# Loading the second pair's keys: two loads of four blocks at steps 5 and 6, then two blocks at every third step

## The chip, the cores and the metric

The kernel runs on one core of one Trainium2 chip. A time is the device time of one execution in microseconds (us). The engines are PE (TensorE, matrix multiplications and transposes), DVE (VectorE), ACT (ScalarE), POOL (GpSimd) and SP (SyncE, which here only starts DMAs). Each engine works through its own list of instructions in order.

## The reference, cut to what matters

Block-sparse attention on 4 batches of 8 heads, 768 positions, 64 channels per head, followed by a token mix:

```python
scores = (q @ k.T) / 8                      # 24 x 24 blocks of 32 x 32 positions
mask = |block_i - block_j| <= 1, or i or j is the first or the last block, or j is one of 3 sampled blocks of i
attn = softmax(where(mask, scores, -1e9))   # x = attn @ v, heads side by side: (4, 768, 512)
theta = x @ w_theta
y = w_tok_r @ (x * cos(theta)) + w_tok_i @ (x * sin(theta))
u = x + y
out = u + relu(u @ w_ch)
```

## The kernel before, in words

**Two pairs.** The four batches are worked as two pairs (`bp` 0 and 1), two batches at a time. A pair has 28 units: six wide units `w` for the two edge rows of blocks, which see all keys (thirds `t` = 0, 1, 2 of the keys, eight blocks each, and two halves `a` of the heads), and then 22 inner units `i` = 1 to 22, one per other row of blocks, each of which sees eight blocks of keys. Unit numbers run through both pairs: 0 to 5 wide and 6 to 27 inner for the first, 28 to 33 wide and 34 to 55 inner for the second.

**Steps.** One loop over `n` runs the units as a pipeline whose order is written by hand. Step `n` does the scores of unit `n + 1` (PE, line 331 for wide and 339 for inner units, tiles `S_w` and `S`), the transposes of unit `n` (line 369, `T_w`, `T`), the products with the values of unit `n - 1` (line 393, `X_w`, `X`), and around them the minimum on DVE (line 342), the exponentials on ACT (line 359) and the normalisation on DVE (lines 400 to 402). Between these, DVE and ACT turn the float64 weights of the token mix into pairs of float32 (lines 63 to 86; the raw weights are loaded from ACT's queue, line 59).

**Keys.** A pair's keys are one tile of 24 blocks (`k0`, `k1`; 128 partitions, 256 float32 per block). The wide units read it directly: a wide unit of third `t` needs blocks `8t` to `8t + 7`. For an inner unit, POOL copies its window and two sampled blocks into `kg` (lines 297 and 276) and ACT the third sampled block (line 279), three steps ahead. The sampled blocks are found by number, so these copies wait for all loads of the tile. The first pair's keys are loaded ahead of the loop. The second pair's tile `k1` has a place of its own and is filled during the first pair's steps by `load_k` (line 231), from SP's queue.

**Values.** For an inner unit the window's rows come into `va` (line 309, SP) and the sampled rows by an indirect DMA into one of four buffers `vb` (line 313, POOL). The second pair's wide units have their values loaded into these same four `vb` buffers by `load_wide` (line 235, SP): two at step 26, two at step 28 and two more at step 30.

**SP's order.** Within a step SP starts, in this order: queries (line 241), window rows (309), a finished result (421), a part of the edge rows' result (438), `load_k`, the edge queries `qe` (257, at step 24), `load_wide`. DMAs of SP and of ACT take the next of eight completion semaphores in turn and wait, when they are started, until the last DMA on that semaphore has landed.

**After the attention** comes the token mix (lines 582 to 702), which is one dense stream of matrix multiplications.

Of the kernel before, what the change touches and what calls it, by code (L numbers as in the profile page):

```python
# [183 lines left out]
def attention(tc, qT, qE, kT, vr, sampled, xs, ident, early_pieces, late_pieces, first_places, follow, spares):  # L184
# [14 lines left out]
    with ExitStack() as ctx, ExitStack() as early:  # L199
# [20 lines left out]
        def make_places(bp):  # L220

            if bp == 0:
                k, v = first_places()
                wide[bp] = [v[:, 1040 * c : 1040 * (c + 1)] for c in range(6)]
            else:
                k = kp.tile([P, 6144], F32, name="k1")
                wide[bp] = vbs + vbs[:2]
            ks[bp] = k.rearrange("r (s g f) -> r s g f", s=NB, g=8)

        def load_k(bp, s0, n, queue=nc.sync):  # L230
            queue.dma_start(ks[bp][:, s0 : s0 + n].rearrange("r s g f -> r s (g f)"), kT[bp][:, s0 : s0 + n])

        def load_wide(bp, t, queue=nc.sync):
            for c in (2 * t, 2 * t + 1):
                queue.dma_start(wide[bp][c], vr[768 * bp + 128 * c : 768 * bp + 128 * c + 128])

        def load_q(bp, i):
            if i % 2 == 0:
                return
            t = qp.tile([P, 2, 2, 4, 32], F32, tag="q", name=f"q{bp}_{i}", bufs=Q_BUFS)  # L240
            nc.sync.dma_start(t.rearrange("r u b p f -> r u (b p f)"), qT[bp][:, i - 1 : i + 1, :])
            qbs[bp, i], qbs[bp, i + 1] = t[:, 0], t[:, 1]
            unscaled[bp, i] = t.rearrange("r u b p f -> r (u b p f)")
# [8 lines left out]
        def scale_edges(bp):  # L252
            scale(qes[bp].rearrange("r b p f -> r (b p f)"))

        def load_edges(bp):
            qes[bp] = ep.tile([P, 2, 4, 64], F32, tag="qe", name=f"qe{bp}")
            nc.sync.dma_start(qes[bp].rearrange("r b p f -> r (b p f)"), qE[bp])
# [41 lines left out]
        def load_window(bp, i):  # L299
            va, runs = vas[i % 2], fresh(i)  # L300
            if i <= 2:
                nc.sync.dma_start(va[96:128], vr[768 * bp : 768 * bp + 32])
            elif i % 3 < 2:

                runs, rows = [(i + 1, 1)], slice(0, 32 * (i % 3) + 32)
                nc.gpsimd.tensor_copy(va[rows], vas[(i + 1) % 2][rows])  # L306
            for b0, n in runs:
                s0 = 32 * (b0 % 3)
                nc.sync.dma_start(va[s0 : s0 + 32 * n], vr[768 * bp + 32 * b0 : 768 * bp + 32 * (b0 + n)])
# [113 lines left out]
        def join(bp, a):  # L423

            xw, f = xws[a], fs[a].rearrange("r t (e b) -> r t b e", e=2)
            for t in range(3):
                nc.gpsimd.tensor_tensor(xw[:, t], xw[:, t], f[:, t].unsqueeze(3).to_broadcast([P, 2, 2, 65]), op=ALU.mult)
                yield
            for t in range(1, 3):
                nc.gpsimd.tensor_tensor(xw[:, 0], xw[:, 0], xw[:, t], op=ALU.add)  # L430
                yield
            rows = xw.rearrange("r t b e d -> r (t b e d)")[:, 260:516]
            normalised(f"{bp}_a{a}", xw[:, 0], rows.rearrange("r (b e d) -> r b e d", b=2, e=2))
            for s_ in range(2):
                for z in range(2):
                    yield
                    r0, p0 = 64 * s_ + 32 * z, 32 * (2 * a + s_)
                    nc.sync.dma_start(xs[bp, p0 : p0 + 32, (NB - 1) * z].rearrange("r b c -> r (b c)"), rows[r0 : r0 + 32])
# [11 lines left out]
        def do(n, stage, *args):  # L450
            if 0 <= n < len(units):
                stage(units[n], *args)

        def inner(n, stage):
            if 0 <= n < len(units) and units[n][1] != "w":
                stage(*units[n][:2])
# [5 lines left out]
        with tc.manual_schedule():  # L462
            load_edges(0)
            make_places(0)
            load_k(0, 0, 8)
            tab = Tables(nc, cp, sampled)

            nc.vector.memset(first, 0.0)
            nc.scalar.activation(first, first, AF.Exp)
            idle = ps_x.tile([P, P], F32, tag="X", name="idle")  # L470
            for _ in range(WARM):
                nc.tensor.matmul(idle, ident, ident, start=True, stop=True)
            decoder = Decoder(early_pieces + late_pieces, stage, nc.scalar)
            load_wide(0, 0)
            load_k(0, 8, 8)
            load_wide(0, 1)
            load_k(0, 16, 8)
            decoder.load(0, nc.sync)
            load_q(0, 1)
            load_wide(0, 2)  # L480
            decoder.load(1, nc.sync)
            load_q(0, 3)
            make_places(1)
            scale_edges(0)
            do(0, scores)
            making = tab.make(nc, cp)
            next(making)
            do(0, weights)
            steps = len(units) + 1
            for n in range(steps):  # L490
                if n == len(units) - 1:
                    early_s.close()
                    next(follow)


                weight = lambda k: sum(4 if u[1] == "w" else 7 for u in units[5:k])
                due = 3 * len(decoder.pieces) * weight(n) // weight(len(units) - 4)
                due = min(due, 3 * len(decoder.pieces)) - decoder.at
                decoder.first_on_scalar(due)
                do(n + 1, scores)  # L500
                next(making, None)
                inner(n + 4, number_blocks)
                inner(n + 3, gather_window)
                inner(n + 3, gather_keys)
                if due > 0:
                    decoder.on_vector()
                if due > 1 and decoder.at % 3:
                    decoder.on_vector()
                do(n, turn)
                do(n - 1, values)  # L510
                if len(units) - 2 <= n < len(units):
                    next(follow)
                do(n, evict)
                do(n + 1, weights)
                inner(n + 3, gather_key)
                inner(n + 3, scale_q)
                decoder.on_scalar()
                do(n - 1, finish)
                if units[min(n + 6, steps - 2)][:2] not in ((0, 1), (0, 3)):
                    inner(n + 6, load_q)  # L520
                inner(n + 2, gather_values)

                inner(n + 1, lambda bp, i: load_window(bp, i) if i > 2 else None)
                inner(n + 3, lambda bp, i: load_window(bp, i) if i <= 2 else None)
                inner(n - 1, store)

                if n <= len(units) and units[n - 1][1:] in (("w", (2, 0)), ("w", (2, 1))):
                    joins.append(join(units[n - 1][0], units[n - 1][2][1]))
                if n % half > 6 and joins and next(joins[0], joins) is joins:
                    joins.pop(0)  # L530
                if 5 <= n < 29 and n % 2:
                    load_k(1, n - 5, 2)
                if n == 24:
                    load_edges(1)
                if n == half - 3:
                    scale_edges(1)
                for t, step in enumerate((half - 2, half, half + 2)):
                    if n == step:
                        load_wide(1, t)

                if n == len(units) - 4:
                    early.close()
                if len(units) - 6 <= n < len(units):
                    next(follow)
            assert not decoder.left() and not joins, (decoder.left(), joins)
# [285 lines left out]
def sparse_attention_then_token_mix(ctx, tc, qT, qE, kT, vr, sampled, w_theta, w_tok_r, w_tok_i, w_ch, outT):  # L831
# [63 lines left out]
    spares = []  # L895
    follow = token_mix(tc, w, last, xs, outT, bias, n_batch, lambda: spares[0]())
    attention(tc, qT, qE, kT, vr, sampled.bitcast(I32), xs, ident, early, late, first_places, follow, spares)
    for _ in follow:
        pass
# [47 lines left out]
```

## Time and profile before

| | |
|---|---|
| three runs | 593.72, 599.39 and 599.77 us, median 599.39 |
| the profiled execution | 595.23 us, its span 593.5 us |
| mean granted TensorE clock | 0.976 |
| busy over the span | PE 92%, PE weight loads 73%, DVE 72%, ACT 57%, POOL 31% |
| queue of SP and queue of POOL | 53.28 MB and 22.85 MB, 29.0% and 14.3% of the DMA engines' time |
| attention, then token mix | until about 248 us, then 345 us |

A span runs from the first to the last instruction; the execution's own time is 1.7 us more. Busy shares are means over stages that have different limits: in the token mix PE alone is near full, in the attention several engines and the DMA engines are. Line numbers are those of the kernel before; in the changed kernel the lines behind the edit stand three lines lower.

### The profile page before, as it was taken

The page shows a single profiled execution, that of the slowest core. Times are in us where ns is not written, and L with a number is a line of the kernel's source. Part 1 is how long each engine was busy: PE and PEld are TensorE (multiplying, and loading weights), DVE is VectorE, ACT ScalarE, POOL GpSimd, SP SyncE. Part 2 cuts the span into 40 slices and gives each one's busy share as a digit, 9 for nine tenths or more (in the row PEclk, how much of TensorE's full clock was granted, in tenths as well). Part 3 has the DMA queues.
Part 4 walks back from the last instruction along what each step waited for, and adds up shares of the span by engine and source line. Part 5 has one row for each costly group of instructions (what it writes and reads, how often), then busy time and mean ns, then how long its engine had stood idle before and what let it go on. Part 6 is the DMA issues. An engine that isn't in the chain of part 4 may idle for free.

```text
span 593.5 us, 17325 instructions
## 1 busy us (share of the span) xinstructions
PE 547.3 (92%) x7092; PEld 434.5 (73%) x7092; DVE 426.5 (72%) x846; ACT 335.3 (57%) x684; POOL 185.6 (31%) x281
## 2 busy tenths in 40 slices
PE   6997786779988888899999999999999999999997
PEld 4775554556645655688888888888888888888886
DVE  3778998978799989879999995657722659614252
ACT  4798687768967878766474562345530446421220
POOL 1389869922588899520000000000000000000000
PEclk9899989889998989999999999999999999999999
DMA  8979999879987988842333132310202311102002
GB/s 311 351 222 270 263 264 253 251 207 313 273 229 211 260 240 225 227 128 76 85 110 87 36 94 86 104 53 8 83 20 80 99 36 35 36 27 81 1 1 106
DMA packets 53087, 86.67 MB, mean 146 GB/s; under 512 B 5392, under 2 KB 31632, under 8 KB 52624
## 3 DMA queue, kind: packets, MB, share of 16 engines
q1 hardware_dynamic: 43200, 53.28, 29.0%
q0 software_dynamic: 6944, 22.85, 14.3%
q10 hardware_dynamic: 2864, 9.44, 5.2%
q8 instruction: 56, 0.92, 0.7%
q14 instruction: 23, 0.19, 0.1%
HBM read 72.95 MB, written 12.58 MB: 144 GB/s over the span
## 4 chain that ended last, share of the span: by engine, by line
PE 73%; DVE 14%; DMA 6%; issue 3%; ACT 2%; SPq 0%; DVEq 0%; ACTq 0%
PE ya L668 23%; PE yb L668 11%; PE T L369 5%; PE S L339 4%; DVE m L342 4%; PE h L609 4%; PE X L393 4%; PE h L612 4%; PE h L610 4%; PE o L693 3%; PE o L694 3%; PE o L695 2%; PE X_w L393 2%; PE T_w L369 2%; DMA k<-in_kT_dram 2%
## 5 line engine op out<-in xcount | busy, mean ns | idle before, releaser
L359 ACT ACTIVATE P<-S,m 128x256 f32<-128x256 f32 x176 | 70.0, 498 | 15.1 <-DVE m L342 13.9
L369 PE MATMUL T<-ident,P 128*128 128x128 f32 x352 | 61.3, 299 | 16.0 <-ACT P L359 12.6
L369 PEld LDWEIGHTS T<-ident,P 128*128 128x128 f32 x352 | 41.2, 146 | 44.7 <-ACT P L359 35.5
L342 DVE TENSOR_REDUCE m<-S 128x4 f32<-128x1024 f32 x44 | 53.5, 1216 | 9.2 <-PE S L339 7.5
L339 PE MATMUL S<-kg,q 64*32 64x256 f32 x1408 | 54.2, 395 | 5.7 <-issue 5.4
L668 PE MATMUL ya<-w_values,zh 128*128 128x512 f32 x160 | 59.4, 395 | 0.0
L375 ACT COPY pT<-T 128x512 f32<-128x512 f32 x88 | 47.8, 599 | 12.9 <-PE T L369 12.6
L393 PE MATMUL X<-vb,pT 128*32 128x65 f32 (+1 forms) x1408 | 48.2, 227 | 6.9 <-issue 6.9
L393 PE MATMUL X<-va,pT 128*32 128x65 f32 (+1 forms) x1408 | 48.8, 230 | 6.1 <-issue 5.5
L313 POOL DMA_INDIRECT vb<-in_vr_dram,rows x44 | 44.5, 1012 | 19.5 <-PE X_w L393 9.2
L297 POOL COPY kg<-k 128x256 f32<-128x256 f32 (+2 forms) x66 | 37.5, 585 | 33.0 <-DMA k<-in_kT_dram 15.9
L668 PE MATMUL ya<-w_keys,zh 128*128 128x512 f32 x128 | 47.6, 396 | 0.0
L276 POOL COPY kg<-k 128x256 f32 x88 | 46.3, 552 | 0.0
L701 DVE SCALAR_TENSOR_TENSOR of<-o,xT 128x512 f32<-128x512 f32 (+1 forms) x24 | 13.3, 557 | 45.7 <-PE o L695 42.5
L393 PEld LDWEIGHTS X<-va,pT 128*32 128x32 f32 (+1 forms) x1408 | 34.1, 114 | 14.7 <-issue 12.2
L668 PE MATMUL yb<-w_values,zh 128*128 128x256 f32 x160 | 44.6, 278 | 0.0
L393 PEld LDWEIGHTS X<-vb,pT 128*32 128x32 f32 (+1 forms) x1408 | 36.2, 115 | 8.7 <-issue 8.6
L306 POOL COPY va<-va 32x1040 f32<-32x1040 f32 (+1 forms) x28 | 32.5, 1160 | 23.3 <-DMA va<-in_vr_dram 13.6
L609 PE MATMUL h<-w_theta_hi,xh 128*128 128x512 f32 x96 | 38.2, 398 | 0.4 <-ACT xh L598 0.4
L625 DVE SCALAR_TENSOR_TENSOR rr<-t,h 128x512 f32<-128x512 f32 x24 | 16.5, 687 | 29.8 <-ACT t L619 29.8
L610 PE MATMUL h<-w_theta_lo,xh 128*128 128x512 f32 x96 | 37.9, 395 | 0.0
L339 PEld LDWEIGHTS S<-kg,q 64*32 64x32 f32 x1408 | 22.8, 108 | 19.1 <-issue 10.3
(175 smaller groups left out, 1460.0 us busy)
## 6 DMA issues: line engine op xcount, KB each, us to landing
va<-in_vr_dram SPq DMA_DIRECT2D x58, 130.0 KB
q<-in_qT_dram SPq DMA_DIRECT2D x22, 256.0 KB
xs<-xo SPq DMA_DIRECT2D x22, 256.0 KB
xr<-xs SPq DMA_DIRECT2D x22, 256.0 KB
xa<-xs SPq DMA_DIRECT2D x88, 64.0 KB
raw_tok_r<-in_w_tok_r_dram ACTq DMA_DIRECT2D x8, 576.0 KB
out_dram<-of SPq DMA_DIRECT2D x16, 256.0 KB
v<-in_vr_dram SPq DMA_DIRECT2D x6, 520.0 KB
```

Of the source, the lines that this page charges most:

```text
L276: nc.gpsimd.tensor_copy(*sampled_keys(bp, i, k))
L297: nc.gpsimd.tensor_copy(kgs[i % 2][:, s0 : s0 + n], ks[bp][:, b0 : b0 + n])
L313: nc.gpsimd.indirect_dma_start(out=vbs[(i + 1) % VB][rows], out_offset=None, in_=vr, in_offset=bass.IndirectOffsetOnAxis(ap=tab.rows[rows, ...
L339: nc.tensor.matmul(sc[32 * p : 32 * p + 32, e, b, :], q[rows, b, p, :], keys[rows, :, 4 * b + p, :], start=True, stop=True)
L342: nc.vector.tensor_reduce(m.rearrange("r (e b) -> r e b", e=2), sc, axis=AX.X, op=ALU.min)
L359: nc.scalar.activation(pt[:, e, b], sc[:, e, b], AF.Exp, bias=m[:, 2 * e + b : 2 * e + b + 1], scale=-1.0)
L369: nc.tensor.transpose(banks[k // 4][:, k % 4], pt[:, (k // 2) % 2, k % 2, 128 * (k // 4) : 128 * (k // 4) + 128], ident)
L375: nc.scalar.copy(out[:, 4 * h : 4 * h + 4], bank)
L393: nc.tensor.matmul(s["X"][rr, b, e, :], s["T"][0:rows, 4 * c + 2 * e + b, rr], v[0:rows, v0 : v0 + 65], start=c == 0, stop=c == 1,)
L609: nc.tensor.matmul(ps, hi[:, c, :], wh[:, c, :], start=c == 0, stop=False)
L610: nc.tensor.matmul(ps, hi[:, c, :], wl[:, c, :], start=False, stop=False)
L668: nc.tensor.matmul(acc, z[:, dd], wt[:, t0 : t0 + n], start=first and (n == 512 or c % 2 == 0), stop=last, skip_group_check=n == 256,)
```

## The change

Before, `k1` comes in twelve loads of two blocks (256 KB each) at the odd steps 5, 7, ... 27. After, it comes in ten: four blocks (512 KB) at step 5 and four at step 6, then two blocks each at steps 8, 11, 14, 17, 20, 23, 26 and 29. The bytes are the same.

```diff
-                if 5 <= n < 29 and n % 2:
-                    load_k(1, n - 5, 2)
+
+                if n in (5, 6):
+                    load_k(1, 4 * n - 20, 4)
+                if 8 <= n < 32 and n % 3 == 2:
+                    load_k(1, 8 + (n - 8) // 3 * 2, 2)
```

No instruction of PE, DVE, ACT or POOL is added, removed or moved. On SP two DMAs fewer are started and the others change places. At the beginning (steps 5 to 8) SP's list is, before, where `k1` is the second pair's key tile, `q0_7` the first pair's queries and `va` a window of values:

```order
L231 DMA k1_160<-in_kT_dram 128x512
L241 DMA q0_7_629<-in_qT_dram 128x512
L309 DMA va1_117<-in_vr_dram 32x1040
L231 DMA k1_160<-in_kT_dram 128x512
L241 DMA q0_9_823<-in_qT_dram 128x512
L309 DMA va0_116<-in_vr_dram 32x1040
L421 DMA xs_73<-xo0_1_722 128x512
L309 DMA va1_117<-in_vr_dram 32x1040 x2
L231 DMA k1_160<-in_kT_dram 128x512
```

and after:

```order
L231 DMA k1_160<-in_kT_dram 128x1024
L241 DMA q0_7_629<-in_qT_dram 128x512
L231 DMA k1_160<-in_kT_dram 128x1024
L309 DMA va1_117<-in_vr_dram 32x1040
L241 DMA q0_9_823<-in_qT_dram 128x512
L309 DMA va0_116<-in_vr_dram 32x1040
L421 DMA xs_73<-xo0_1_723 128x512
L231 DMA k1_160<-in_kT_dram 128x512
L309 DMA va1_117<-in_vr_dram 32x1040 x2
```

The first two loads are twice as wide, the second has moved ahead of a window load, and the third stands ahead of the next pair of window loads.

At the other end (steps 25 to 30) SP's list is, before, where the `vb` are the values of the second pair's wide units and `q1` the second pair's queries:

```order
L231 DMA k1_160<-in_kT_dram 128x512
L309 DMA va0_116<-in_vr_dram 32x1040
L421 DMA xs_73<-xo0_19_2480 128x512
L438 DMA xs_73<-xw0_w01_346 32x256
L235 DMA vb0_118<-in_vr_dram 128x1040
L235 DMA vb1_119<-in_vr_dram 128x1040
L231 DMA k1_160<-in_kT_dram 128x512
L241 DMA q1_1_2719<-in_qT_dram 128x512
L421 DMA xs_73<-xo0_21_2645 128x512
L235 DMA vb2_120<-in_vr_dram 128x1040
L235 DMA vb3_121<-in_vr_dram 128x1040
L241 DMA q1_3_2837<-in_qT_dram 128x512
```

and after:

```order
L309 DMA va0_116<-in_vr_dram 32x1040
L421 DMA xs_73<-xo0_19_2478 128x512
L438 DMA xs_73<-xw0_w01_346 32x256
L231 DMA k1_160<-in_kT_dram 128x512
L235 DMA vb0_118<-in_vr_dram 128x1040
L235 DMA vb1_119<-in_vr_dram 128x1040
L241 DMA q1_1_2716<-in_qT_dram 128x512
L421 DMA xs_73<-xo0_21_2643 128x512
L235 DMA vb2_120<-in_vr_dram 128x1040
L235 DMA vb3_121<-in_vr_dram 128x1040
L231 DMA k1_160<-in_kT_dram 128x512
L241 DMA q1_3_2835<-in_qT_dram 128x512
```

The last key load, which brings blocks 22 and 23, stood between `vb1` and `vb2`; now it stands behind `vb3`.

On PE the order is the same. At step 31 it reads, before, with the semaphores that each instruction waits for (`DMAHW` are the eight of the DMAs; 7 and 0 are here those of the key loads of steps 27 and 25, 3 and 4 those of `vb2` and `vb3`):

```order
L331 MATMUL S_w_2841<-k_160,qe_2403 64x256 [waits DMAHW7_49,DMAHW0_49,DVE_49]
L331 MATMUL S_w_2841<-k_160,qe_2403 64x256 x7
L369 MATMUL T_w_0_2869<-ident,P_w_2830 128x128 [waits PE_49,Activation_49]
L369 MATMUL T_w_0_2869<-ident,P_w_2830 128x128 [waits Activation_49] x3
L369 MATMUL T_w_1_2870<-ident,P_w_2830 128x128 [waits PE_49]
L369 MATMUL T_w_1_2870<-ident,P_w_2830 128x128 x3
L393 MATMUL X_w_2879<-vb_120,pT_w_2827 64x65 [waits DMAHW3_49,DVE_49]
L393 MATMUL X_w_2879<-vb_120,pT_w_2827 64x65
L393 MATMUL X_w_2879<-vb_121,pT_w_2827 64x65 [waits DMAHW4_49]
```

and after:

```order
L331 MATMUL S_w_2839<-k_160,qe_2401 64x256 [waits DMAHW5_49,DMAHW6_49,DMAHW2_49,DVE_49]
L331 MATMUL S_w_2839<-k_160,qe_2401 64x256 x7
L369 MATMUL T_w_0_2867<-ident,P_w_2828 128x128 [waits PE_49,Activation_49]
L369 MATMUL T_w_0_2867<-ident,P_w_2828 128x128 [waits Activation_49] x3
L369 MATMUL T_w_1_2868<-ident,P_w_2828 128x128 [waits PE_49]
L369 MATMUL T_w_1_2868<-ident,P_w_2828 128x128 x3
L393 MATMUL X_w_2877<-vb_120,pT_w_2825 64x65 [waits DMAHW0_49,DVE_49]
L393 MATMUL X_w_2877<-vb_120,pT_w_2825 64x65
L393 MATMUL X_w_2877<-vb_121,pT_w_2825 64x65 [waits DMAHW1_49]
```

The scores of unit 32, the first of the last third of the keys, now wait for semaphore 2, which is that of the load of step 29; they stand ahead of the product that needs `vb2` and `vb3`.

## The prediction

> **What bounds the kernel now.** I read the page first: PE is busy for 92% of the span, but DMAs can only matter where others wait for them. So the busy times by stage come next (per engine us and count, then granted clock, DMA share, GB/s).
>
> ```profile
> core 0: us, PE busy (x) PEld busy (x) DVE busy (x) ACT busy (x) POOL busy (x), PEclk, DMA share, GB/s
> 26.00:44.00 18.00, 17.91 (x439) 12.64 (x432) 13.14 (x24) 17.74 (x46) 13.04 (x20) 1.00 0.80 231
> 44.00:64.00 20.00, 15.39 (x491) 10.63 (x495) 17.43 (x33) 15.65 (x36) 19.32 (x29) 1.00 0.98 265
> ...
> 132.00:152.00 20.00, 19.54 (x409) 14.36 (x408) 16.52 (x32) 16.82 (x40) 5.04 (x10) 0.91 0.93 297
> 152.00:248.00 96.00, 81.29 (x2201) 54.15 (x2194) 87.57 (x151) 76.51 (x180) 80.56 (x115) 0.96 0.85 236
> 248.00:593.00 345.00, 340.42 (x1960) 291.66 (x1959) 218.75 (x469) 145.74 (x242) 11.65 (x20) 1.00 0.22 66
> ```
>
> The last 345 us are PE's token mix, with DMAs at 0.22; the change cannot touch them except by moving their start. From 152 to 248 us DVE is busy for 91% of the time: it sets the pace there, and DVE time that goes unused just before is not won back. The key loads fall between 26 and 135 us; the two stages at its head have the DMA engines 0.80 and 0.98 occupied. The turn from the first pair to the second, 132 to 152 us, belongs to PE (19.54 of 20 us). The chain that ended last shows where a DMA stands on the path there (start, us, what):
>
> ```profile
> 114.28 8.56 DMA raw_tok_r<-in_w_tok_r_dram
> ...
> 122.85 4.07 DMA qe<-in_qE_dram
> ...
> 140.20 6.73 DMA vb<-in_vr_dram
> ...
> 148.01 1.00 PE S_w L331 x13
> ```
>
> The first piece (weights, then edge queries behind them on one semaphore) is not changed by the edit: neither issue moves past the other. The second is the load of `vb3`, which lands at 146.93 us and is waited for by the product of unit 30.
>
> **The last load, step 29.** These are PE and SP around it, in order of time:
>
> ```profile
> 140.82 1.09 PE L331 MATMUL S_w<-k,qe 64*64 64x256 f32 x16
> 141.84 1.09 PE L369 MATMUL T_w<-ident,P_w 128*128 128x128 f32 x8
> 142.86 1.15 PE L393 MATMUL X_w<-vb,pT_w 128*64 128x65 f32 x32
> 143.94 1.09 PE L331 MATMUL S_w<-k,qe 64*64 64x256 f32 x16
> 144.97 1.27 PE L369 MATMUL T_w<-ident,P_w 128*128 128x128 f32 x8
> ...
> 146.97 1.04 PE L393 MATMUL X_w<-vb,pT_w 128*64 128x65 f32 x28 [0.46 <-DMA vb<-in_vr_dram]
> ```
>
> ```profile
> 133.31 0.42 SPq L231 DMA_DIRECT2D k<-in_kT_dram  x1
> ...
> 139.20 0.33 SPq L421 DMA_DIRECT2D xs<-xo  x1
> 139.70 0.87 SPq L235 DMA_DIRECT2D vb<-in_vr_dram  x2
> 140.67 0.53 SPq L241 DMA_DIRECT2D q<-in_qT_dram  x1
> ```
>
> The scores at 143.94 us are unit 32's, the first that read blocks 16 to 23. Before, their last load was issued at 133.31 us and was in long since. After, it takes the place of the query load at 140.67 us, because SP cannot pass the result store of 139.20 us and the two `vb` loads. The 256 KB then stand behind `vb3` on the same queue. At this stage's 297 GB/s they need 0.88 us, so I put their landing at 146.93 + 0.88 = 147.8 us, and the scores at 147.85 instead of 143.94 us. PE works in order: scores, transposes and the product (1.02 + 1.02 + 1.08 us from the starts at 140.82, 141.84, 142.86 and 143.94) then put the next scores at 150.97 us, against 148.01 in the chain. That is **+3.0 us**. The wait for `vb3` that was there (0.46 us) vanishes into it. Bounds: as fast as the 4.07 us of `qe`, the load would land at 144.7 us, and the product would still wait for `vb3`: 0. As slow as the 8.56 us of the weights, it lands at 149.2 us: +4.4. I take 3.0, because the row nearest to it is `vb3` itself, issued just ahead on the same queue. Behind the waiting scores on PE stand all later scores; DVE's minimum and ACT's exponentials wait for them, and with them the DVE-bound stage.
>
> POOL waits for the same load:
>
> ```profile
> 138.53 0.40 POOL L297 COPY kg<-k 128x256 f32<-128x256 f32 x1 [8.44 <-DMA k<-in_kT_dram]
> ...
> 141.61 1.27 POOL L276 COPY kg<-k 128x256 f32 x2
> 151.31 1.02 POOL L313 DMA_INDIRECT vb<-in_vr_dram,rows  x1 [8.43 <-PE X_w L393]
> ```
>
> Its 4.4 us of copies move from 138.5 to 147.8 us and end at 152.2; the gather behind them moved to about 154.3 with PE, so this costs nothing. ACT's copy of the third sampled block stands behind unit 32's exponentials, which wait anyway.
>
> **The clock after the gap.** PE would stand still for 3.9 us. Stretches of 3.4 us, and what clock the next one had:
>
> ```profile
> 111.50:114.90 3.40, 1.42 (x7) 0.85 (x8) 3.30 (x8) 2.06 (x6) 3.23 (x5) 1.00 0.85 292
> 114.90:118.30 3.40, 3.40 (x91) 2.47 (x97) 3.30 (x7) 3.40 (x9) 2.94 (x6) 0.50 0.93 274
> 125.20:128.60 3.40, 1.51 (x38) 0.89 (x37) 0.36 (x1) 1.66 (x4) 1.23 (x2) 1.00 0.69 169
> 128.60:135.40 6.80, 5.95 (x92) 3.99 (x88) 5.73 (x12) 5.34 (x13) 1.44 (x2) 0.50 0.62 184
> 53.50:56.90 3.40, 1.76 (x81) 1.05 (x71) 2.52 (x6) 3.23 (x8) 3.24 (x6) 1.00 1.04 279
> 56.90:60.30 3.40, 3.37 (x110) 2.44 (x109) 2.59 (x3) 2.12 (x6) 3.40 (x5) 1.00 1.00 325
> ```
>
> With PE busy for 1.42 and 1.51 of 3.4 us the next stretch ran at 0.50; with 1.76 it stayed at 1.00. However a gap of 3.9 us falls across such stretches, one of them has at most 3.4 - 1.95 = 1.45 us of work. So I expect one stretch at half clock, in which a PE that never rests loses half of 3.4 us: **+1.7 us**. Bounds: 0, if PE's stretch hides under ACT, and 3.4, if it lasts for 6.8 us as at 128.60. I take the single stretch, as after 111.50.
>
> The Trainium skill, "TensorE: Matmul & The Clock Gate", Part 1, says that the clock falls to half after at least one idle window of about 3.4 us, and that windows run freely. By that rule a gap of 3.9 us rarely holds a whole window, and the sum would be +2.0 us, the first of the rivals below. The rows at 111.50 and 125.20 speak against it: neither stretch was idle throughout.
>
> **The first loads, steps 5 and 6.** By 28 us 1024 KB are issued where there were 256, 768 KB more, 3.4 us of queue at that stage's 231 GB/s. The second load passes a window load that SP holds back until PE frees its buffer:
>
> ```profile
> 38.62 0.33 SPq L309 DMA_DIRECT2D va<-in_vr_dram  x1
> 38.99 0.95 SPq L231 DMA_DIRECT2D k<-in_kT_dram  x1
> ```
>
> The stage around it, in the columns of the first table:
>
> ```profile
> 34.00:42.00 8.00, 8.00 (x266) 6.06 (x272) 6.30 (x12) 8.00 (x20) 7.06 (x13) 1.00 0.66 178
> ```
>
> Between 34 and 42 us the DMA engines are only 0.66 occupied, 2.7 us free, and the load of 38.99 us is gone; so the burst fits almost whole into a hole. Cost 0; if it does not fit, one stall of PE such as the 1.83 us below: 0 to +1.8.
>
> **The middle, steps 7 to 25.** Ten loads become six, 1024 KB less, and those of steps 8, 14 and 20 pass ahead of window loads. What could be won are PE's stalls for which the profile shows no releaser:
>
> ```profile
> 45.10 1.83 issue
> 46.93 0.50 PE X L393 x18
> ...
> 55.26 1.67 issue
> ...
> 61.92 1.08 issue
> ...
> 96.62 1.86 issue
> ```
>
> SP had issued key loads at 38.99 us (above) and at
>
> ```profile
> 48.23 0.44 SPq L231 DMA_DIRECT2D k<-in_kT_dram  x1
> ...
> 94.16 0.42 SPq L231 DMA_DIRECT2D k<-in_kT_dram  x1
> ```
>
> and the page has of the queues (packets, MB, share):
>
> ```profile
> q8 instruction: 56, 0.92, 0.7%
> ```
>
> The first falls inside a group of equal matmuls (18 of 64 are left at 46.93 us), so no semaphore is late. The instruction queue moved 0.92 MB in the span, so code comes in over the same DMA engines, and I read these stalls as PE waiting for its code behind data. Those at 45.10, 55.26 and 96.62 us come some 2 to 7 us behind a key load that is gone; each could shrink by 256 KB at 265 GB/s, 1.0 us, so at most -3.0, and at least 0, since loads elsewhere move closer to other fetches. I take **-1.0**, one of three. Two DMAs fewer on SP, 0.4 us each, are worth 0: SP mostly waits.
>
> The Trainium skill, "DMA: Bandwidth & Descriptors", Queues, rings and completion order, says that each DMA engine takes turns between queues packet by packet. Then code does not stand behind a backlog of keys, the middle wins nothing, and the sum is 1.0 higher. No row here shows where a fetch stood.
>
> **The sum.** +3.0 + 1.7 + 0 - 1.0 = +3.7 us on the profiled execution's 595.2 us gives 598.9. That execution lies 4.2 us below the median of 599.39; it and the three runs (593.72 to 599.77) have a mean of 597.0, and I predict from there: **600.7 us**. A change within 1%, 6 us, can hardly be told from none here.
>
> **Rivals**, each as a difference from before.
> - *Full clock*: the gap comes without the half clock, or ACT hides it: 3.0 - 1.0 = +2.0, 599.0 us. For it: the limit between 1.51 and 1.76 us of work is read from few stretches. Chance 0.17.
> - *No relief*: a fetch of code does not stand behind keys, so the middle wins nothing: +4.7, 601.7 us. For it: the stall at 61.92 us comes though no key load that goes stands shortly ahead of it. Chance 0.12.
> - *Faster*: the load of step 29 overtakes (0, no half clock), and the three stalls go altogether (1.83 + 1.67 + 1.86): -5.4, 591.6 us. For it: DMAs at 0.98 from 44 to 64 us, where 512 KB leave; against it, a load would have to overtake two on its own queue. Chance 0.12.
> - *Slower*: the burst is late. If PE's code misses its place behind 1 MB around 40 us (+1.8) and a second half-clock stretch follows there (+1.7), with the step-29 wait at its upper end (4.4 + 1.7) and no relief, +9.6, 606.6 us. It decides once the 768 KB take more than the 2.7 free us. Chance 0.19.
>
> **How the numbers follow.** The forecast has 0.40. All but the faster and slower cases lie within 1%; around them a run's scatter of 3 us puts some over. Slower by over 1%: most of the slower case and a little of the forecast and of no relief, 0.23. Faster: two thirds of its case, 0.08. Within: 0.69. The range leaves out about half of the two outer cases: 593.5 to 606.5 us.
>
> **What would show it.** PE's `S_w` of unit 32 waits for `DMA k<-in_kT_dram` for about 4 us near the turn, POOL's wait for the keys grows from 8.4 to about 17 us, and the clock of the next 3.4 us is 0.50. The stalls at 45.10 and 55.26 us shrink or not. I am wrong if unit 32's scores start within 1 us of the transposes' pace, or if a new wait stands between 28 and 44 us.

## The result, and the profile after

| | before | changed |
|---|---|---|
| first comparison, 20 executions each: median | 595.12 us (588.94 to 599.94) | 601.88 us (597.32 to 606.63) |
| mean | 595.26 us | 601.80 us |
| the profiled execution, its span, mean clock | 595.23, 593.5 us, 0.976 | 604.64, 602.9 us, 0.968 |

The ratio (changed over before) is 1.014 with a 95% interval of 1.011 to 1.017. Two later comparisons, each on a chip of its own and run with the experiments below, gave 1.0037 (1.0004 to 1.0071) and 1.0096 (1.0054 to 1.0138). The changed kernel is slower in all three; the size is not steady. The plain mean of the three ratios is 1.009, 5.4 us on 595. Ratios leave disturbed executions out, so they can differ from the quotient of two medians.

The stages of the changed kernel, in the columns of the prediction's first table (busy us of each engine and count, granted clock, DMA share, GB/s):

```profile
core 0: us, PE busy (x) PEld busy (x) DVE busy (x) ACT busy (x) POOL busy (x), PEclk, DMA share, GB/s
26.00:44.00 18.00, 16.67 (x466) 12.12 (x469) 13.12 (x22) 16.69 (x42) 13.62 (x23) 1.00 0.91 291
44.00:64.00 20.00, 14.56 (x360) 9.54 (x360) 14.92 (x31) 13.85 (x34) 16.92 (x26) 0.91 0.82 229
...
132.00:152.00 20.00, 16.24 (x326) 12.30 (x328) 12.30 (x25) 12.61 (x30) 3.35 (x9) 0.87 0.91 304
152.00:248.00 96.00, 75.09 (x2007) 51.18 (x2006) 83.14 (x139) 72.24 (x173) 73.77 (x109) 0.96 0.79 216
248.00:602.00 354.00, 349.59 (x2235) 298.36 (x2233) 227.68 (x487) 153.64 (x261) 16.09 (x25) 1.00 0.23 70
```

The edit's first half shows in the DMA columns: 0.91 instead of 0.80 up to 44 us, 0.82 instead of 0.98 after it. In the same two stages PE is busy for 16.67 us where it was 17.91, and for 14.56 where it was 15.39, and the clock from 44 to 64 us is 0.91 where it was 1.00. At the turn, 132 to 152 us, PE is busy for 16.24 us where it was 19.54, and every other engine is less busy with it. PE, then SP, then POOL around the load of step 29 (start, duration, what, and in brackets the idle time before it and what ended it):

```profile
142.19 1.15 PE L393 MATMUL X_w<-vb,pT_w 128*64 128x65 f32 x32
147.11 1.86 PE L331 MATMUL S_w<-k,qe 64*64 64x256 f32 x16 [3.76 <-issue]
148.90 1.95 PE L369 MATMUL T_w<-ident,P_w 128*128 128x128 f32 x8
...
151.87 1.09 PE L331 MATMUL S_w<-k,qe 64*64 64x256 f32 x16
```

```profile
139.03 0.88 SPq L235 DMA_DIRECT2D vb<-in_vr_dram  x2
139.96 0.57 SPq L231 DMA_DIRECT2D k<-in_kT_dram  x1
```

```profile
147.07 0.40 POOL L297 COPY kg<-k 128x256 f32<-128x256 f32 x1 [16.20 <-DMA k<-in_kT_dram]
...
155.24 1.01 POOL L313 DMA_INDIRECT vb<-in_vr_dram,rows  x1 [4.81 <-PE X_w L393]
```

SP starts the last key load right behind `vb2` and `vb3`. POOL's copy, which waits for all of `k1`, starts at 147.07 us, and unit 32's scores at 147.11 us. The trace names no releaser for the 3.76 us on PE ("issue"), but POOL is released by the key load 0.04 us earlier, and the same wait is put down to the key load in the experiments with that load alone. Behind it, scores and transposes take 1.86 and 1.95 us where they took 1.09: the clock was halved.

```profile
143.88:147.29 3.41, 0.18 (x4) 0.21 (x8) 0.37 (x2) 0.55 (x2) 0.22 (x1) 1.00 1.03 409
147.29:150.71 3.42, 3.42 (x24) 2.23 (x19) 1.63 (x4) 0.58 (x1) 3.13 (x9) 0.50 1.04 298
```

From unit 31's scores to unit 33's it takes 11.72 us (140.15 to 151.87), against 7.12 before (140.82 to 147.94): +4.6 us. The execution is 9.4 us longer than the profiled one of before, so as much again lies elsewhere. PE's waits without a releaser, in total, times and longest, are after

```profile
PE X L393 <- issue: 16.9, 12, 2.8
PE S L339 <- issue: 10.3, 6, 3.7
...
PE T L369 <- issue: 2.8, 1, 2.8
```

and before

```profile
PE X L393 <- issue: 12.5, 11, 2.4
...
PE S L339 <- issue: 5.4, 4, 2.5
```

that is 30.0 against 17.9 us, each of them one execution; the wait for the key load is not counted in. Whether that belongs to the change had to be tested.

### The profile page after: what moved, and what is told of

It is laid out like the page before. It is cut to its first block, busy times and chain, and to the rows that moved or that the text cites. A ratio compares the mean times of both kernels' runs of the same rounds, so it can differ in the third digit from the quotient of the medians.

```text
span 602.9 us, 17322 instructions
## 1 busy us (share of the span) xinstructions
PE 547.8 (91%) x7092; PEld 437.3 (73%) x7092; DVE 424.3 (70%) x846; ACT 334.4 (55%) x684; POOL 177.8 (29%) x281
## 4 chain that ended last, share of the span: by engine, by line
PE 76%; DVE 10%; issue 6%; DMA 3%; ACT 3%; SPq 1%; DVEq 0%; ACTq 0%
PE ya L671 22%; PE yb L671 11%; PE T L369 7%; PE X L393 6%; PE S L339 6%; PE h L612 4%; PE h L615 4%; PE h L613 4%; PE o L696 3%; PE o L697 2%; DMA k<-in_kT_dram 2%; PE o L698 2%; DVE m L342 2%; PE S_w L331 1%; ACT P L359 1%
## 5 line engine op out<-in xcount | busy, mean ns | idle before, releaser
L359 ACT ACTIVATE P<-S,m 128x256 f32<-128x256 f32 x176 | 69.8, 496 | 17.2 <-DVE m L342 16.9
L369 PEld LDWEIGHTS T<-ident,P 128*128 128x128 f32 x352 | 42.5, 151 | 41.6 <-ACT P L359 30.9
L339 PE MATMUL S<-kg,q 64*32 64x256 f32 x1408 | 55.0, 406 | 10.3 <-issue 10.3
L393 PE MATMUL X<-va,pT 128*32 128x65 f32 (+1 forms) x1408 | 50.7, 234 | 9.4 <-issue 9.4
L393 PE MATMUL X<-vb,pT 128*32 128x65 f32 (+1 forms) x1408 | 49.7, 232 | 7.5 <-issue 7.4
L297 POOL COPY kg<-k 128x256 f32<-128x256 f32 (+2 forms) x66 | 36.2, 565 | 47.0 <-DMA k<-in_kT_dram 23.2
L393 PEld LDWEIGHTS X<-va,pT 128*32 128x32 f32 (+1 forms) x1408 | 35.2, 116 | 16.3 <-issue 14.5
L276 POOL COPY kg<-k 128x256 f32 x88 | 41.9, 502 | 0.0
L306 POOL COPY va<-va 32x1040 f32<-32x1040 f32 (+1 forms) x28 | 30.8, 1101 | 27.2 <-DMA va<-in_vr_dram 18.2
```

What stands on the lines that cost most here:

```text
L276: nc.gpsimd.tensor_copy(*sampled_keys(bp, i, k))
L297: nc.gpsimd.tensor_copy(kgs[i % 2][:, s0 : s0 + n], ks[bp][:, b0 : b0 + n])
L339: nc.tensor.matmul(sc[32 * p : 32 * p + 32, e, b, :], q[rows, b, p, :], keys[rows, :, 4 * b + p, :], start=True, stop=True)
L359: nc.scalar.activation(pt[:, e, b], sc[:, e, b], AF.Exp, bias=m[:, 2 * e + b : 2 * e + b + 1], scale=-1.0)
L369: nc.tensor.transpose(banks[k // 4][:, k % 4], pt[:, (k // 2) % 2, k % 2, 128 * (k // 4) : 128 * (k // 4) + 128], ident)
L393: nc.tensor.matmul(s["X"][rr, b, e, :], s["T"][0:rows, 4 * c + 2 * e + b, rr], v[0:rows, v0 : v0 + 65], start=c == 0, stop=c == 1,)
```

## The experiments

**The theory**: the cost is the last key load behind `vb2` and `vb3`, with the half clock that follows. **The rivals**: the burst (the wide loads of steps 5 and 6), or the loads that it moves, make PE's code late; or no part costs anything that can be told from scatter. The kernels came in three groups of four, each on one chip with its own executions of the kernel before.

**First group** (before: median 598.47 us). *The burst without the late load:*

```diff
-                if 5 <= n < 29 and n % 2:
+                if n in (5, 6):
+                    load_k(1, 4 * n - 20, 4)
+                if 13 <= n < 29 and n % 2:
```

> The kernel before, with its first four key loads (steps 5, 7, 9, 11) replaced by two of four blocks at steps 5 and 6; steps 13 to 27 as before. Theory A (the turn alone: the scores of unit 32 wait for the last load, +3.0, and the clock then halves, +1.7): same as before, within 1.5 us. Theory B (the burst of 1 MB makes PE's code late at about 48 us and at 62 us, as in the changed kernel's profile): +2 to +4 us, with a PE stall of over 2.5 us between 40 and 66 us.

Ratio 1.0037 (0.9992 to 1.0081), median 601.39 us: not clear of none.

*The late load without the burst:*

```diff
-                if 5 <= n < 29 and n % 2:
-                    load_k(1, n - 5, 2)
+                if 5 <= n < 27 and n % 2 or n == 29:
+                    load_k(1, min(n, 27) - 5, 2)
```

> The kernel before, with its last key load alone (blocks 22 and 23) moved from step 27 to step 29, behind the loads of vb2 and vb3. Theory A: +4.7 us or the whole measured difference of about 7; POOL's wait for the keys grows to about 16 us, and the scores of unit 32 start 3 to 4 us later than the pace, with the next 3.4 us at clock 0.50. Theory B: at most +2.

Ratio 1.0074 (1.0029 to 1.012), median 602.39 us: slower. At the turn its profiled execution (605.01 us, the longest of its twelve) names the releaser:

```profile
145.18 1.15 PE L393 MATMUL X_w<-vb,pT_w 128*64 128x65 f32 x32
149.23 1.09 PE L331 MATMUL S_w<-k,qe 64*64 64x256 f32 x16 [2.90 <-DMA k<-in_kT_dram]
150.26 1.09 PE L369 MATMUL T_w<-ident,P_w 128*128 128x128 f32 x8
```

Here the wait is 2.90 us instead of 3.76, and the clock stayed full behind it: the groups take 1.09 us.

*The change with its last load back at step 27, ahead of `vb2`:*

```diff
-                if 8 <= n < 32 and n % 3 == 2:
-                    load_k(1, 8 + (n - 8) // 3 * 2, 2)
+                if 8 <= n < 29 and n % 3 == 2 or n == 27:
+                    load_k(1, 22 if n == 27 else 8 + (n - 8) // 3 * 2, 2)
```

> The changed kernel, with its last key load moved back from step 29 to step 27, between vb1 and vb2; all other loads as changed. Theory A: back at before, or up to 1 us under it by the thinner middle. Theory B: still +2 to +4 over before. POOL's wait for keys falls to about 8 us in either.

Ratio 1.0041 (0.9996 to 1.0086), median 601.22 us. The turn is as before: PE waits for no key,

```profile
143.81 1.04 PE L393 MATMUL X_w<-vb,pT_w 128*64 128x65 f32 x28 [0.64 <-DMA vb<-in_vr_dram]
144.77 1.09 PE L331 MATMUL S_w<-k,qe 64*64 64x256 f32 x16
...
147.90 1.09 PE L331 MATMUL S_w<-k,qe 64*64 64x256 f32 x16
```

and unit 32's scores follow unit 31's by 3.13 us. The time, however, did not come back whole: what is left over is -0.2 to +5.1 us.

*The change with 48 more score matmuls ahead of unit 32's scores* (three times the scores of the first third, overwritten by the real ones), to keep PE working in the gap:

```diff
                 q, keys = qes[bp], ks[bp][:, 8 * t : 8 * t + 8]
+                for _ in range(3 if (bp, t, a) == (1, 2, 0) else 0):
+                    for b, s_, e in [(b, p, e) for b, p, e in heads if p < 2]:
+                        rows, p = slice(64 * e, 64 * e + 64), 2 * a + s_
+                        nc.tensor.matmul(sc[...], q[rows, b, p, :], ks[bp][rows, 0:8, 4 * b + p, :], start=True, stop=True)
```

> The changed kernel with 48 extra score matmuls (unit 32's queries on blocks 0 to 7, overwritten by its own scores right after) ahead of unit 32's scores, so that PE works for 3.1 us of the 3.8 that it waits for the last load. Theory A with the clock term: the scores start at the same time, but the clock behind them stays at 1.00, and the time is 1.5 to 2 us under the changed kernel. Rival (the half clock costs nothing since ACT or DVE set the pace there): same as the changed kernel or up to 0.5 us more.

Ratio 1.014 (1.0087 to 1.0192) from eight executions (plain means: 603.08 us against 598.74 before), though at the turn it did what was meant (L332 are the added matmuls, L335 the scores, L373 the transposes):

```profile
143.46 2.82 PE L332 MATMUL S_w<-k,qe 64*64 64x256 f32 x48
147.12 1.09 PE L335 MATMUL S_w<-k,qe 64*64 64x256 f32 x16 [0.84 <-DMA k<-in_kT_dram]
148.15 1.09 PE L373 MATMUL T_w<-ident,P_w 128*128 128x128 f32 x8
...
150.25 1.09 PE L335 MATMUL S_w<-k,qe 64*64 64x256 f32 x16
```

Full clock behind the wait, and 9.92 us from unit 31's scores (140.33) to unit 33's, 1.8 less than the changed kernel's 11.72. The whole time did not show it; it was run again below.

**Second group** (before: median 599.68 us). *The changed kernel once more:*

> The changed kernel once more, on the chip of the next three. Theory A2 (two costs add up: the late load, +4.4 by its run alone, and the burst, +2.4 by the two runs that have it): +6 to +8 over before, clock under 0.95 between 44 and 64 us. Rival (the burst's +0.4% was scatter): +4 to +5.

Ratio 1.0037 (1.0004 to 1.0071), well under the first 1.014. The turn is the same again:

```profile
142.83 1.09 PE L331 MATMUL S_w<-k,qe 64*64 64x256 f32 x16
...
149.96 1.98 PE L331 MATMUL S_w<-k,qe 64*64 64x256 f32 x16 [3.93 <-issue]
151.87 1.73 PE L369 MATMUL T_w<-ident,P_w 128*128 128x128 f32 x8
...
154.61 1.09 PE L331 MATMUL S_w<-k,qe 64*64 64x256 f32 x16
```

*Twice the burst, and no late load:*

```diff
-                if 5 <= n < 29 and n % 2:
+                if n in (5, 6):
+                    load_k(1, 8 * n - 40, 8)
+                if 21 <= n < 29 and n % 2:
```

> The kernel before, with eight blocks at step 5 and eight at step 6 (2 MB) in place of eight loads of two, then two blocks at steps 21, 23, 25 and 27 as before. Theory A2 (a burst delays PE's code): +4 to +8, with longer stalls of PE without releaser between 36 and 66 us than the 1.8 us of before, and the clock halved there. Rival (the burst is free, the hole at 34 to 42 us takes it, or the bytes saved later pay for it): within 1.5 of before.

Ratio 0.9977 (0.9937 to 1.0018), median 598.25 us. Two megabytes in the two loads cost nothing that can be told, and in this execution PE worked through them (same columns as the stages above):

```profile
26.00:34.00 8.00, 7.99 (x162) 5.51 (x152) 4.63 (x10) 7.90 (x22) 3.90 (x6) 1.00 1.03 342
34.00:42.00 8.00, 7.74 (x181) 5.46 (x178) 5.47 (x10) 7.49 (x18) 5.99 (x12) 1.00 0.86 298
```

With the DMA engines full to 34 us PE is busy for 7.99 of 8 us. The +4 to +8 us that the rival of the burst asked for lie outside the interval. A smaller cost is not excluded: this kernel also loads no keys from step 7 to step 20, which could pay for it.

*The kernel before with its last load at step 28, one place ahead of `vb2` and `vb3`:*

```diff
-                if 5 <= n < 29 and n % 2:
-                    load_k(1, n - 5, 2)
+                if 5 <= n < 27 and n % 2 or n == 28:
+                    load_k(1, min(n, 27) - 5, 2)
```

> The kernel before, with its last key load moved to step 28, right ahead of the loads of vb2 and vb3 (in the run with it at step 29 it stood right behind them). Theory A (what costs is standing behind 1 MB on the same queue): unit 32's scores wait for at most 0.5 us, vb3 lands 0.9 us later, the time is 0 to +1.5 over before. Rival (what costs is the later step as such, or the scatter): +3 to +5 as with step 29.

Ratio 1.0006 (0.9964 to 1.0048). Two places on SP's queue separate it from the slower kernel with step 29:

```profile
143.48 0.42 SPq L231 DMA_DIRECT2D k<-in_kT_dram  x1
144.08 0.92 SPq L235 DMA_DIRECT2D vb<-in_vr_dram  x2
```

```profile
148.04 1.09 PE L331 MATMUL S_w<-k,qe 64*64 64x256 f32 x16
...
151.56 1.04 PE L393 MATMUL X_w<-vb,pT_w 128*64 128x65 f32 x28 [1.14 <-DMA vb<-in_vr_dram]
```

Unit 32's scores (148.04 us) wait for nothing: the load was in within 4.56 us of its issue. Behind the two `vb` loads it took 7.15 us in the changed kernel (139.96 to 147.11), so it is the place on the queue that counts, and not the later step. The price is a wait for `vb3` of 1.14 us instead of 0.46.

*All twelve loads at steps 14 to 25:*

```diff
-                if 5 <= n < 29 and n % 2:
-                    load_k(1, n - 5, 2)
+                if 14 <= n < 26:
+                    load_k(1, 2 * n - 28, 2)
```

> The kernel before, with the twelve loads of two blocks at every step from 14 to 25, none ahead. Theory A2 (queues that are full at 26 to 64 us make PE's code late): the stalls between 40 and 64 us shrink, clock there 1.00, time 0 to -3. Rival (DVE sets the pace from 64 us on, so early time is not won, and the loads now crowd the weights and edge queries at 114 to 127 us): 0 to +3, with a longer wait for qe than 5.0 us.

Ratio 1.0039 (1.0000 to 1.0078), no wait for the last load, `vb3` waited for 0.27 us. Nothing gained, perhaps something lost.

**Third group** (before: median 597.88 us), to have the disputed sizes side by side. *The changed kernel a third time, the late load alone again, and the added matmuls again:*

> The changed kernel once more, as the measure for the other three on the same chip. Its ratio to the kernel before was 1.014 the first time and 1.0037 the second. If the cost is the wait at the turn alone (+3 to +4.7 us), the ratio is 1.005 to 1.008; if there is a second cost of the size of the first result, it is above 1.011; if there is none to be measured, it is within 0.003 of 1. In the profile unit 32's scores wait for 2.9 to 3.9 us in every case.

> The kernel before with its last load alone moved from step 27 to step 29. Theory A (the cost of the whole change is this load, which stands behind vb2 and vb3): the same time as the changed kernel on this chip, within 2 us, and 3 to 5 us over the kernel before. Rival B (the two loads of four blocks, or the loads moved between them, cost as well): 2 us or more below the changed kernel. Rival C (nothing that can be measured): within 1.5 us of the kernel before.

> The changed kernel with 48 more score matmuls ahead of unit 32's scores, into the same tile and overwritten by it, so that PE works in the gap. If the half clock after the gap carries 1.7 us of the cost, this kernel is 1.5 to 2 us faster than the changed kernel on the same chip, since the extra work of 2.8 us fits into the wait of 3 to 4 us. If the half clock is hidden under the other engines, it is the same within 1 us. If the extra matmuls don't fit into the wait, it is slower.

Ratios 1.0096 (1.0054 to 1.0138), 1.0083 (1.0044 to 1.0121) and 1.0073 (1.0034 to 1.0112), means 602.56, 601.28 and 600.79 us against 597.49 before. The late load alone is 3.8 us over before and 1.3 us under the whole change, with an uncertainty of 2.1 on the latter. The added matmuls bring 1.8 us against the whole change, also with an uncertainty of 2.1: of the size at the turn, but not resolved. The late load alone, and then the added matmuls, at the turn:

```profile
146.27 1.98 PE L331 MATMUL S_w<-k,qe 64*64 64x256 f32 x16 [3.91 <-DMA k<-in_kT_dram]
148.19 1.76 PE L369 MATMUL T_w<-ident,P_w 128*128 128x128 f32 x8
```

```profile
144.26 2.82 PE L332 MATMUL S_w<-k,qe 64*64 64x256 f32 x48
148.06 1.09 PE L335 MATMUL S_w<-k,qe 64*64 64x256 f32 x16 [0.98 <-DMA k<-in_kT_dram]
```

*A candidate, all keys in by step 19:*

```diff
-                if 5 <= n < 29 and n % 2:
-                    load_k(1, n - 5, 2)
+                if n in (5, 6):
+                    load_k(1, 8 * n - 40, 8)
+                if 13 <= n < 21 and n % 2:
+                    load_k(1, n + 3, 2)
```

> A candidate: eight blocks each at steps 5 and 6, then two each at steps 13, 15, 17 and 19, so that no key load stands among the values of the second pair's wide units at steps 26 to 29. Theory A (only the end of the keys' order matters, and a burst is free): S_w of unit 32 has no wait for k, and the wait for vb3, 0.46 us before, is gone or smaller; 0 to 1.5 us faster than the kernel before. Rival B (a burst costs PE its code): 2 to 4 us slower than before. Rival D (loads moved from steps 21 to 27 into steps 13 to 19 delay what is loaded there): slower by 1 us or more, with a new wait for va, kg or qe between 70 and 125 us.

Ratio 1.0014 (0.9973 to 1.0054), the same as before. The wait for `vb3` is not smaller without a key load near it:

```profile
147.93 1.04 PE L393 MATMUL X_w<-vb,pT_w 128*64 128x65 f32 x28 [0.51 <-DMA vb<-in_vr_dram]
```

No order that was tried is measurably faster than the one before.

From unit 31's scores to unit 33's, read alike from every trace: with the last load behind `vb3` 11.72, 11.78 and 11.84 us (the changed kernel) and 11.80 (the late load alone) with a halved clock, 9.23 (the late load alone, first group) without; with the added matmuls 9.92 and 10.06; with the last load anywhere ahead of `vb2` 7.12 (before), 7.11, 7.08, 7.62, 6.75 and 6.98. In the change with its last load at step 27 the wait for values lies one unit earlier; there units 30 to 33 take 10.34 us, against 10.25 before.

## Why the prediction was right, and where it was not

**The last load: right, mechanism and size.** Forecast: unit 32's scores 7.03 us behind unit 31's (140.82 to 147.85); measured 6.96 (140.15 to 147.11). POOL's wait was to grow from 8.44 to about 17 us and is 16.20, free of cost as said: POOL still waits 4.81 us for PE ahead of its gather. That the order on SP's queue decides is shown from both sides: the load alone makes the kernel slower twice (1.0074, 1.0083), and two places further ahead it costs nothing (1.0006).

**The half clock: right at the turn, in four of five executions.** Forecast +3.0 and +1.7 us across the turn; measured +4.6 to +4.7 where the clock fell. Where it stayed full, the late load alone cost 2.1 us there (9.23 against 7.12), but there the gap was 2.90 us, and its emptiest stretch held 1.56 us of work. The four gaps of 3.76 to 3.97 us, which is what the prediction reckoned with, were all followed by the half clock, so nothing here bears out the rival *Full clock* for a gap of that length. The clock's share of the whole time (the added matmuls: 1.8 us at the turn, -1.8 with an uncertainty of 2.1 in the mean) agrees but is not resolved.

The Trainium skill, "TensorE: Matmul & The Clock Gate", Part 1, asks for an idle window of about 3.4 us ahead of the half clock. Three of the four halved turns agree (a whole stretch with at most 0.18 us of work). The fourth does not: the stretch ahead of its half clock held 0.89 us of work, as the last section shows.

**The burst: 0 is not refuted, and not shown.** Kernels with eight blocks a load are not slower (0.9977, 1.0014), and four blocks alone (1.0037, 0.9992 to 1.0081) cannot be told from none. But the prediction named a new wait between 28 and 44 us as a sign of being wrong, and the profiled execution of the changed kernel has one:

```profile
35.78 0.26 PE L393 MATMUL X<-va,pT 96*32 96x65 f32 x3 [0.84 <-issue]
```

The profiled execution of the third comparison has 0.56 us at this place, that of the second nothing. That is inside the bounds of 0 to +1.8 us. The prediction's own figures did not speak for a plain 0 either: it put the added loads at 3.4 us of queue and the room for them at 2.7.

**The middle: wrong, the step "I take -1.0".** It took three single stalls to be owed to single loads ahead of them. In the profiled execution of the changed kernel these three did shrink, by more than was forecast: the one of 45.10 us from 1.83 to 0.32, the one of 55.26 from 1.67 to none, the one of 96.62 from 1.86 to 0.85. But others grew at other places of PE's list, and the sum went from 17.9 to 30.0 us. PE in that execution, around the first two places:

```profile
43.49 0.24 PE L393 MATMUL X<-vb,pT 128*32 128x65 f32 x1 [0.32 <-issue]
...
51.60 1.92 PE L339 MATMUL S<-kg,q 64*32 64x256 f32 x29 [3.68 <-issue]
...
56.32 1.09 PE L339 MATMUL S<-kg,q 64*32 64x256 f32 x32
...
64.92 0.22 PE L393 MATMUL X<-va,pT 128*32 128x65 f32 x1 [2.58 <-issue]
```

The scores at 56.32 us are those that stood still ahead of their last six in the kernel before. In the profiled executions of the second and the third comparison they stand still at that very place again, for longer:

```profile
59.09 0.63 PE L339 MATMUL S<-kg,q 64*32 64x256 f32 x6 [2.42 <-issue]
```

```profile
57.79 1.07 PE L339 MATMUL S<-kg,q 64*32 64x256 f32 x6 [5.16 <-issue]
```

The three stalls together are 5.4 us before and 1.2, 4.0 and 7.7 us in the three profiled executions of the changed kernel. So the place of a stall is fixed and its length is not, and one execution could not price it. The change without its late load, in which the -1.0 stands alone if the burst is free, came out at 1.0041 (0.9996 to 1.0086), so the gain lies just outside the interval. Without the term the sum is +4.7 us, the rival *No relief*, which is nearest to the mean ratio of 1.009; the 1.014 of the first comparison alone is nearest to *Slower* (+9.6 us).

**The level: too high, which hid the rest.** 600.7 us was +3.7 on a mean of 597.0 from four executions. In the first comparison the kernel before ran at 595.3 us on average and the difference was 6.5 us; the two errors cancel in the time (601.8 against the forecast 600.7), not in the difference. That the time came so near is in part luck. From one comparison to the next the median before was 595.1, 598.5, 599.7 and 597.9 us, so four executions could not place it better.

**What stays open.** The turn explains 4.6 us, and the late load alone costs 0.7 to 0.8% by the ratios, 2.9 and 3.8 us by the plain means. Of the first comparison's difference (6.5 us by the means, 8.3 by the ratio) 2 to 4 us are not explained; the second comparison (0.4%) has no such surplus, on the third chip the whole change is 1.3 us over the late load alone with an uncertainty of 2.1, and the change without its late load is 0.4% over before, just within its uncertainty.

The wide loads of steps 5 and 6 remain a suspect. Among the twelve profiled executions under 605 us, PE's waits without a releaser on `S`, `T` and `X` come to 16.3 to 30.0 us in the eight with these loads, five of them above 24, and to 15.6 to 20.8 us in the four without; the clock between 44 and 64 us is below 1.00 in five of the eight and in one of the four. That is the mechanism of the rival *Slower*, late code and a second half clock, though mostly behind 44 us and not around 40. Against it stand the times: the two kernels with the largest such loads are not slower, and one of them has 26.7 us of these waits. So a cost of the burst is neither shown nor excluded.

## What to carry to other kernels

A transfer that is needed first must stand first on its queue: here 256 KB, moved from ahead of two 520 KB loads to behind them, made PE stand still for 4 us (about 3 of them lost, since a wait for the values goes) and, through the clock, cost some 1.8 us more at the turn, though it was issued 3.4 us before PE came to it (139.96 to 143.35). How early and how coarsely the rest is loaded made no difference that could be resolved, as long as each piece came before its need. A single stall in one execution is not yet a cost that an edit can remove: look at the same instruction in a second execution, and at the sum over all stalls, before pricing it.

## What the runs showed of the hardware

**The clock.** Its changes lie a multiple of 3.41 us apart in every trace, so each trace can be cut into stretches at them. The clock's fall does not need a stretch without work. In the changed kernel on the third chip the stretch ahead held 0.89 us of PE's work and the next ran at half clock:

```profile
147.35:150.77 3.42, 0.89 (x16) 0.60 (x16) 0.00 (x0) 0.00 (x0) 0.93 (x3) 1.00 1.05 416
150.77:154.18 3.41, 3.41 (x36) 2.87 (x34) 2.05 (x4) 1.78 (x4) 2.42 (x7) 0.50 1.06 283
```

The prediction's 1.51 us (halved) and 1.76 us (full) suggest a limit between them. There is none in busy time alone. In the kernel before, a stretch with 2.06 us of work was followed by the half clock, and one with 1.54 us was not:

```profile
73.96:77.37 3.41, 2.06 (x38) 0.95 (x21) 3.31 (x8) 3.07 (x9) 2.38 (x5) 1.00 0.92 249
77.37:80.79 3.42, 3.42 (x91) 2.50 (x97) 3.14 (x7) 3.42 (x9) 1.52 (x2) 0.50 0.84 220
```

```profile
91.03:94.44 3.41, 1.54 (x74) 1.31 (x82) 3.10 (x7) 3.41 (x9) 3.30 (x6) 1.00 0.93 319
94.44:97.85 3.41, 2.18 (x65) 1.45 (x45) 2.98 (x4) 2.48 (x7) 3.34 (x4) 1.00 1.00 246
```

Counted over the attention (the first 262 us) in all fourteen traces, the 59 stretches at full clock with under 1.52 us of work were all followed by the half clock. Of those with 1.52 to 2.24 us, 31 were and 87 were not, and above that none was. What decides between the two is not shown. So work put into a long wait can keep the clock: 2.82 us of matmuls whose result is not used, inside a wait of some 4 us, did so in both executions.

**The waits for code.** PE's waits without a releaser weigh 12.5 and 5.4 us on `X` and `S` before and 16.9 and 10.3 after, single ones up to 5.2 us. The traces bear out the prediction's reading of them. Before and after, the instruction queue carries 56 packets of 16 KB, for PE's 7,092 matmuls and as many weight loads: one packet for some 253 of them. The waits of over 0.3 us in the kernel before stand a multiple of 126 matmuls apart in PE's list, to within one, and 126 matmuls with their weight loads are 252. And each of these fourteen waits ends 1.2 to 1.7 us after such a packet has ended. In the changed kernel 19 of 20 do; the twentieth, 3.3 us after one, is the wait for the key load. The Trainium skill, "Runtime: NRT & Kernel Launch", Instruction fetch mechanics, says that engine code comes in blocks of 16 KiB over a DMA queue of its own and that this is mostly hidden. The size agrees; hidden it is not here. What makes a packet late, data on other queues or something else, no run shows.
